# A hyena filter and a maxout feed-forward block: the down product of two tiles by Strassen's method

## The chip, the cores and the metric

The kernel runs on one core of one Trainium2 chip. Its time is the device time of one execution in microseconds. A profiled execution is read beside it: TensorE (PE) multiplies matrices, VectorE (DVE), ScalarE (ACT) and GpSimd (POOL) work elementwise, SyncE (SP) issues most of the DMAs.

## The reference

```python
# x, v: (4, 12544, 128); float32 throughout
h_mlp = np.maximum(pos_emb @ w1, 0.0) @ w2
h_filt = h_mlp * np.exp(-0.01 * np.arange(S))[:, None]
u = x * v
y = irfft(rfft(u, n=2*S, axis=1) * rfft(h_filt, n=2*S, axis=0)[None], n=2*S, axis=1)[:, :S]
t = (x * y).reshape(50176, 128)                 # d_model 128
h = np.maximum(np.maximum(t @ moe_w1, t @ moe_w2), t @ moe_w3)   # d_ff 768
out = h @ moe_w_out                             # (50176, 128)
```

A long convolution along the sequence, for each of four batches, gates `x`; every token then goes through a feed-forward block whose hidden layer is the maximum of three products.

## The kernel before

**The convolution** is a Fourier transform in steps, each a matrix product. The inputs of a batch come in 32 pieces (`u_load`, 128 x 392 of `xr` and of `vr`). A piece is multiplied on VectorE (`u_mul`), split into its 16-bit halves on GpSimd (`u_planes`, L356), turned by a transposing DMA (`u_dma`, tile `turned`), joined again on ScalarE and VectorE (`u_join`, tile `uT`) and multiplied by the first table (`u_first`, L141). Then come 45 pairs of frequencies: tables (`w_load`, tile `wt`) and the filter's spectrum (`h_load`, tile `ht`) are loaded, a second product is taken (`g_second`), VectorE and ScalarE form the sums and the products with the filter (`g_butterfly`, `g_swap`, `g_re`, L419, `g_im`, L423, whose last addition, L424, is on GpSimd, and `g_unfold`, L431), a third product follows (`g_third`), and its result goes to DRAM (`zd`, L450, issued by ScalarE).

**The feed-forward block** works on tiles of 392 tokens (`N`), 32 for each batch, 128 in all. `t_load` brings the tile's part of `zd` (tile `zt`) and of `x` (tile `xT`, four DMAs), `t_last` does the last product of the transform (`yps`) and multiplies by `x` (tile `gt`). Then there are six chunks of 128 hidden channels, one for each up step. The maximum of three is taken as relu of differences: the weights w2 and w3 have w1 subtracted, and what w1 itself contributes goes straight to the output through one 128x128 matrix, `lin`, which is w1 times w_out. An up step (`up`) is a product `pa`, a ReLU on ScalarE into `hid` (L545), a product `pb`, and a maximum on VectorE (L548); `pa` and `pb` turn through the three PSUM buffers of the pool `hps`. The down product (`down`) adds the chunk's share to `ops`; it follows one up step behind. After six chunks ScalarE copies `ops` out (L561) and issues the output's DMA (L563).

Every product is done in two halves of 64 output rows:

```python
    def halves_mm(out, lhsT, rhs, start, stop):
        for h in range(2):
            nc.tensor.matmul(out[64 * h:64 * h + 64], lhsT[:, 64 * h:64 * h + 64], rhs,
                             start=start, stop=stop, skip_group_check=True)
```

**The order** is written by hand; each engine keeps the order in which the program names its instructions. Batch 0 is transformed first, alone. Then the 32 x 6 = 192 up steps of batch b run with the convolution of batch b + 1 beside them: `conv_steps` gives each of its steps a slot, which is the number of an up step. With `per_pair` = 170/(45 + 0.6 x 32) = 2.65 slots, pieces are 1.59 slots apart and pairs of frequencies 2.65; the pieces take about the first 60 slots of a batch (for batch 1 six of them are done earlier), the pairs the others. A piece is loaded 10 slots before its `u_first`, multiplied 6, split 5 and turned 4 slots before, and joined just before. The last batch has nothing beside it.

SyncE's queue holds, in program order, `ut`, `turned`, `wt`, `ht`, `zt` and `xT`. The pieces' tiles come from two pools, `inp` (three buffers) and `inq` (two); `wt` has three buffers for each of its two tags, `ht` three, `uT` two; the convolution's products have four PSUM buffers (`cps`).

Of the kernel before, what the change touches and what calls it, by code (L numbers as in the profile page):

```python
# [9 lines left out]
FP32 = mybir.dt.float32  # L10
# [60 lines left out]
def kernel(  # L71
# [43 lines left out]
    w_sb = [const.tile([D, DFF], FP32, name=f"w_sb{i}") for i in range(3)]  # L115
    wo_sb = const.tile([P, NF, D], FP32, name="wo_sb")
    lin = const.tile([D, D], FP32, name="lin")
    eye = const.tile([P, P], FP32, name="eye")
# [104 lines left out]
    inp = ctx.enter_context(tc.tile_pool(name="inp", bufs=3))  # L223
# [3 lines left out]
    lwp = pro.enter_context(tc.tile_pool(name="lwp", bufs=3))  # L227
    fin = ExitStack()
# [20 lines left out]
    warm = sml.tile([P, 256], FP32, name="warm")  # L249
# [26 lines left out]
    def warm_up(n):  # L276

        ps = fps.tile([P, 1024], FP32, tag="cv", name="pw", bufs=2)
        for _ in range(n):
            halves_mm(ps[:, 0:256], warm[:, 0:P], warm[:], True, True)  # L280
# [34 lines left out]

    NU = NG
    us, uts, ws, hts, eos, xts, xss, abs_, pss = ({} for _ in range(9))

    def pools(b, u):
        if b == 0:  # L320
            return inp0 if u % 2 else inp
        return inp if u < EARLY or u % 5 < 3 else inq

    def u_load(b, u):
        c, g0 = divmod(u, NG // 4)
        ts = []
        for src in (xr, vr):
            t = pools(b, u).tile([P, 4, NB], FP32, tag=f"u{len(ts)}", name="ut")
            nc.sync.dma_start(
                t[:], src[4 * g0:4 * g0 + 4, :, c, b, :].rearrange("g p n -> p g n"))  # L330
            ts.append(t)
        us[u] = ts

    def u_mul(u):
        a, v = us[u]
        nc.vector.tensor_tensor(out=a[:], in0=a[:], in1=v[:], op=ALU.mult)  # L336
# [6 lines left out]
    def u_turn(u):  # L343
        if u % 2 == 0:
            uts[u] = uts[u + 1] = utp.tile([NB, 8, 2, 64], FP32, tag="uT", name="uT")
        ps = state["turn"].tile([P, 512], FP32, tag="cv", name="pst")
        turn(u, ps)
        nc.scalar.copy(uts[u][:, 4 * (u % 2):4 * (u % 2) + 4],
                       ps[0:NB, :].rearrange("n (s t r) -> n s r t", s=4, r=2))
# [3 lines left out]
    def u_planes(u):  # L353
        a, _ = us.pop(u)
        pl_ = planes[u % 3]
        nc.gpsimd.tensor_copy(  # L356
            pl_[:, :, :, 0:NB], a[:].bitcast(U16).rearrange("p s (n h) -> p h s n", h=2))
        us[u] = pl_

    def u_dma(u):  # L360
        t = hp.tile([P, 8, P], U16, tag="turned", name="turned", bufs=3)
        nc.sync.dma_start_transpose(
            out=t[:], in_=us.pop(u)[:].rearrange("p h s n -> p (h s n)"))
        us[u] = t

    def u_join(u):
        if u % 2 == 0:
            uts[u] = uts[u + 1] = utp.tile([NB, 8, 2, 64], FP32, tag="uT", name="uT")
        t = us.pop(u)
        for h in range(2):  # L370
            copies[h](
                uts[u][:, 4 * (u % 2):4 * (u % 2) + 4].rearrange(
                    "n s r t -> n (s r t)").bitcast(U16).rearrange(
                    "n (s r t h) -> n h s r t", h=2, r=2, t=64)[:, h],
                t[0:NB, 4 * h:4 * h + 4].rearrange("n s (t r) -> n s r t", r=2))
# [8 lines left out]
    def w_load(g, a):  # L384

        w = state["pair"][0].tile([P, 2, 2, P], FP32, tag=f"w{a}", name="wt")
        nc.sync.dma_start(w[:].rearrange("p k r m -> p (k r m)"), wt_d[g, :, a, :])
        ws[g, a] = w

    def h_load(g):  # L390
        ht = state["pair"][1].tile([P, 2, 2, 2, D], FP32, tag="h", name="ht")
# [18 lines left out]
    def g_swap(g):  # L410
        xt = xts[g]
        xs = state["cv"][0].tile([P, 2, 2, D], FP32, tag="xs", name="xs", bufs=2)
# [40 lines left out]
    def conv_steps(b, done):  # L453
# [4 lines left out]
        def at(slot, late, fn, *args):  # L458
            out.append((slot, late, len(out), fn, args))
# [14 lines left out]
        for g in range(NK):  # L474
            s = s0 + int(g * per_pair)
            at(s - 5, 0, w_load, g, 0)
            at(s - 3, 0, h_load, g)
# [16 lines left out]
    zts, xTs, gs, pos_, obs = ({} for _ in range(5))  # L494
# [18 lines left out]
    def t_last(i):  # L513
        zt = zts.pop(i)
        ps = cps.tile([P, 512], FP32, tag="cv", name="yps")
        g = hp.tile([D, 4, NB], FP32, tag="g", name="gt", bufs=2)
# [23 lines left out]
    def up(i, f):  # L540
        rhs = gs[i][:].rearrange("d p n -> d (p n)")
        h = hp.tile([P, N], FP32, tag="hid", name="hid")
# [8 lines left out]
    def down(i, f, h):  # L551
        if f == 0:
            pos_[i] = ops.tile([D, 512], FP32, tag="ops", name="ops")
            halves_mm(pos_[i][:, 0:N], lin[:], gs[i][:].rearrange("d p n -> d (p n)"), True,
                      False)
        halves_mm(pos_[i][:, 0:N], wo_sb[:, f, :], h[:], False, f == NF - 1)
        if f < NF - 1:
            return
        gs.pop(i)
        o = op_.tile([D, 4, NB], FP32, tag="o", name="ot")  # L560
        nc.scalar.copy(o[:].rearrange("d p n -> d (p n)"), pos_.pop(i)[:, 0:N])  # L561
        dst = outT.rearrange("d (p b n) -> d p b n", b=B, n=NB)[:, 4 * i[1]:4 * i[1] + 4, i[0], :]
        nc.scalar.dma_start(dst, o[:])  # L563
# [24 lines left out]
    def turn2(u):  # L588

        t = utp.tile([NB, 8, 2, 64], FP32, tag="uT", name="uT")  # L590
# [3 lines left out]
        nc.scalar.copy(t[:], ps[0:NB, :].rearrange("n (s t r) -> n s r t", s=8, r=2))  # L594
# [6 lines left out]
    warm_up(30)  # L601
# [56 lines left out]
    state = {"cv": (cvp, cps), "turn": cps, "xb": 2}  # L658
# [91 lines left out]
    hp = ctx.enter_context(tc.tile_pool(name="hp", bufs=3))  # L750
    f4p = hp.tile([N1, 2, NB // 2], FP32, name="f4p", bufs=1)
    nc.scalar.dma_start(f4p[:], f4p_d)
    inq = ctx.enter_context(tc.tile_pool(name="inq", bufs=2))
    planes = [hp.tile([P, 2, 4, P], U16, name=f"planes{i}", bufs=1) for i in range(3)]
    for t in planes:
        nc.gpsimd.memset(t[:].rearrange("p h s n -> p (h s n)"), 0)
    op_ = ctx.enter_context(tc.tile_pool(name="op", bufs=2))
    wp = ctx.enter_context(tc.tile_pool(name="wp", bufs=3))
    hh = ctx.enter_context(tc.tile_pool(name="hh", bufs=3))
    cvp = ctx.enter_context(tc.tile_pool(name="cvp", bufs=3))  # L760
    cps = ctx.enter_context(tc.tile_pool(name="cps", bufs=4, space=PSUM))
    hps = ctx.enter_context(tc.tile_pool(name="hps", bufs=3, space=PSUM))
    ops = ctx.enter_context(tc.tile_pool(name="ops", bufs=1, space=PSUM))
    state = {"turn": cps, "pair": (wp, hh), "cv": (cvp, cps), "xb": 3}


    tiles = [(b, i) for b in range(B) for i in range(NT)]
    late = None
    for n, (b, i) in enumerate(tiles):
# [4 lines left out]
        if n == 0:  # L774
            t_load(*tiles[0])
            t_load(*tiles[1])
            t_last(tiles[0])
        for f in range(NF):

            if i < NT - 2:  # L780
                if f == 0:
                    t_load(*tiles[n + 2])
            elif i == NT - 1 and f < 2 and n + 1 + f < len(tiles):
                t_load(*tiles[n + 1 + f])
            h = up((b, i), f)
            if late is not None:
                down(*late)
            late = ((b, i), f, h)
            if f == 3 and n + 1 < len(tiles):
                t_last(tiles[n + 1])  # L790
            s = i * NF + f
            run(beside.pop(s, ()))
            if s == NT * NF - 1:
                assert not beside, sorted(beside)
    down(*late)


# [35 lines left out]
```

## Time and profile before

| | us |
|---|---|
| median of 3 runs | 2412.57 |
| lowest and highest | 2412.53, 2420.22 |
| the profiled execution | 2411.47 |
| its span, first to last instruction | 2409.3 |

The first batch's transform, the filter and the weights take about the first 320 us; then come three batches of tiles with a convolution beside them, and from about 1960 us on the last batch alone. In a row of the page's groups stand the line, the engine, the operation, output and inputs with their shapes and the count; behind the bar the busy time in us and the mean of one instruction in ns, then the idle time of the engine before these instructions and what ended most of it. A product of float32 tiles appears as two matmul instructions for each half, so one `halves_mm` is four instructions; their durations overlap each other. A timeline row holds the start, the duration, the engine (SPq and ACTq are the queues from which DMAs are issued), the line and the tile. A row of windows holds the busy time of each engine in a stretch, then TensorE's granted clock, the mean busy share of the DMA engines and GB/s.

### The profile page before, as it was taken

Reading aid. Unit: us, or ns where it says so; the run is one execution under the profiler, and the core shown is the slowest. Engines: PE = TensorE matmul, PEld = TensorE weight load, DVE = VectorE, ACT = ScalarE, POOL = GpSimd, SP = SyncE. Lnnn points to the kernel's source line nnn. Section 1 sums busy time; section 2 is a strip of 40 time slices with the busy share of each in tenths; the row PEclk is TensorE's granted clock in tenths of the full one; section 3 lists DMA queues with packets and bytes.
Section 4 is the critical chain, followed back from the end, with each engine's and each line's share of the span. In section 5 each row is a group of like instructions: output and inputs, shape, how many; then the busy total and the mean of one; then the engine's idle time right before and its main releaser. Section 6 shows DMA issues by size and latency. Waiting matters only on the chain.

```text
span 2409.3 us, 63290 instructions
## 1 busy us (share of the span) xinstructions
PE 2393.4 (99%) x26089; PEld 1463.2 (61%) x26089; DVE 1286.4 (53%) x2719; ACT 1026.7 (43%) x1981; POOL 314.2 (13%) x349
## 2 busy tenths in 40 slices
PE   9999999999999999999999999999999999999999
PEld 8988866655555556666656546666665654444444
DVE  5588834466666645446666644446666642222222
ACT  2688834444444434444444424444444432222222
POOL 2022211011111101101111111101111100000000
PEclk9999999999999999999999999999999999999999
DMA  7778879767767659967777859968777742222221
GB/s 171 179 240 266 278 167 179 162 190 196 214 194 211 175 125 187 182 174 207 219 207 215 219 124 182 189 162 213 214 215 209 215 113 61 55 62 53 64 53 36
DMA packets 544553, 408.21 MB, mean 169 GB/s; under 512 B 390244, under 2 KB 436381, under 8 KB 544265
## 3 DMA queue, kind: packets, MB, share of 16 engines
q1 hardware_dynamic: 421760, 315.25, 53.8%
q10 hardware_dynamic: 117129, 74.31, 10.7%
q0 software_dynamic: 5376, 14.62, 2.1%
q8 instruction: 205, 3.36, 0.6%
q14 instruction: 83, 0.68, 0.1%
HBM read 295.76 MB, written 84.67 MB: 158 GB/s over the span
## 4 chain that ended last, share of the span: by engine, by line
PE 97%; DMA 1%; ACT 1%; DVE 0%; issue 0%; SPq 0%; ACTq 0%; POOL 0%; DVEq 0%
PE ops L132 24%; PE pb L132 21%; PE pa L132 21%; PE ps L132 13%; PE ps L141 7%; PE yps L132 5%; PE sps L688 3%; PE pm L303 1%; PE gps L674 1%; PE pst L341 1%; PE pw L132 1%; DMA hd<-ht 1%; ACT ht L693 0%; DMA xT<-in_x_dram 0%; DVE xt L424 0%
## 5 line engine op out<-in xcount | busy, mean ns | idle before, releaser
L548 DVE TENSOR_TENSOR hid<-hid,pb 128x392 f32<-128x392 f32 x768 | 431.8, 562 | 789.4 <-PE pb L132 510.2
L545 ACT ACTIVATE hid<-pa 128x392 f32<-128x392 f32 x768 | 381.9, 498 | 799.3 <-PE pa L132 630.1
L132 PE MATMUL pa<-gt,w_sb 128*64 128x392 f32 x3072 | 640.7, 493 | 1.1 <-DVE gt L533 1.1
L132 PE MATMUL pb<-gt,w_sb 128*64 128x392 f32 x3072 | 639.6, 492 | 1.4 <-ACT hid L545 1.2
L132 PE MATMUL ops<-hid,wo_sb 128*64 128x392 f32 x3072 | 639.5, 492 | 0.1
L132 PEld LDWEIGHTS pb<-gt,w_sb 128*64 128x64 f32 x3072 | 225.8, 137 | 283.0 <-issue 257.1
L132 PEld LDWEIGHTS ops<-hid,wo_sb 128*64 128x64 f32 x3072 | 227.1, 137 | 278.9 <-issue 228.8
L424 POOL TENSOR_TENSOR xt<-xt,xs 128x512 f32<-128x512 f32 x135 | 172.5, 1278 | 969.6 <-DVE xs L423 778.7
L132 PEld LDWEIGHTS pa<-gt,w_sb 128*64 128x64 f32 x3072 | 201.8, 137 | 111.3 <-issue 67.4
L141 PEld LDWEIGHTS ps<-f,uT 98*64 98x64 f32 x4096 | 178.0, 137 | 47.4 <-issue 44.7
L132 PEld LDWEIGHTS ps<-ab,wt 128*64 128x64 f32 x2880 | 168.4, 137 | 52.4 <-issue 26.8
L132 PE MATMUL ps<-ab,wt 128*64 128x128 f32 x2880 | 190.9, 274 | 1.8 <-DVE ab L431 1.7
L132 PEld LDWEIGHTS ps<-spec,wt 128*64 128x64 f32 x2880 | 168.0, 137 | 37.8 <-issue 34.2
L132 PE MATMUL ps<-spec,wt 128*64 128x128 f32 x2880 | 189.5, 273 | 1.4 <-issue 1.4
L141 PE MATMUL ps<-f,uT 98*64 98x90 f32 x4096 | 188.0, 241 | 0.0
L449 DVE TENSOR_TENSOR zs<-ps,z 128x256 f32<-128x256 f32 x270 | 102.0, 419 | 96.6 <-ACT z L447 94.3
L413 ACT ACTIVATE xs<-xt 64x512 f32<-64x512 f32 x180 | 113.1, 628 | 71.1 <-DVE xt L158 58.9
L431 DVE TENSOR_TENSOR ab<-xt 128x256 f32<-128x256 f32 x360 | 136.0, 419 | 1.6
L419 DVE TENSOR_TENSOR xt<-xt,ht 128x512 f32<-128x512 f32 x180 | 124.2, 690 | 15.6 <-ACT ht L693 15.2
L356 POOL COPY planes<-ut 128x784 uint16<-128x784 uint16 x90 | 76.2, 847 | 426.5 <-DVE ut L336 301.1
L145 ACT COPY spec<-ps 128x360 f32<-128x360 f32 (+1 forms) x132 | 71.8, 546 | 137.0 <-PE ps L141 136.8
L132 PEld LDWEIGHTS yps<-f4p,zt 90*64 90x64 f32 x3072 | 107.3, 138 | 34.4 <-issue 32.3
(86 smaller groups left out, 1824.4 us busy)
## 6 DMA issues: line engine op xcount, KB each, us to landing
wt<-wt_const SPq DMA_DIRECT2D x360, 256.0 KB, 4.8
ht<-hd SPq DMA_DIRECT2D x270, 256.0 KB, 4.5
zd<-zs ACTq DMA_DIRECT2D x180, 256.0 KB, 4.6
zt<-zd SPq DMA_DIRECT2D x192, 180.0 KB, 3.8
ut<-in_xr_dram SPq DMA_DIRECT2D x128, 196.0 KB, 3.6
ut<-in_vr_dram SPq DMA_DIRECT2D x128, 196.0 KB, 4.3
xT<-in_x_dram SPq DMA_DIRECT2D x512, 49.0 KB, 3.0
out_dram<-ot ACTq DMA_DIRECT2D x128, 196.0 KB, 4.0
```

The costliest lines, as they stand in the source:

```text
L132: nc.tensor.matmul(out[64 * h:64 * h + 64], lhsT[:, 64 * h:64 * h + 64], rhs, start=start, stop=stop, skip_group_check=True)
L141: nc.tensor.matmul(ps[64 * c:64 * c + 64, 256 * i + r * N1:256 * i + (r + 1) * N1], a[:, r, :], table[:, c * N1:(c + 1) * N1], start=(i % ...
L145: copy(dst, ps[:].rearrange("p (s m) -> p s m", m=256)[:, :, 0:2 * N1].rearrange("p s (r k) -> p k r s", r=2))
L356: nc.gpsimd.tensor_copy(pl_[:, :, :, 0:NB], a[:].bitcast(U16).rearrange("p s (n h) -> p h s n", h=2))
L413: nc.scalar.mul(xs[0:64], xt[64:128], -1.0)
L419: nc.vector.tensor_tensor(out=xt[:], in0=xt[:], in1=hts[g][:, 0], op=ALU.mult)
L424: (nc.gpsimd if apart else nc.vector).tensor_tensor(out=xt[:], in0=xt[:], in1=xs[:], op=ALU.add)
L431: nc.vector.tensor_tensor(out=ab[:, :, q, :], in0=y[:, :, 0, :], in1=y[:, :, 1, :], op=op)
L449: nc.vector.tensor_tensor(out=zs[:, a], in0=ps[:, 0:256], in1=z1[:], op=op)
L545: nc.scalar.activation(h[:], pa[:, 0:N], Relu)
L548: nc.vector.tensor_tensor(out=h[:], in0=h[:], in1=pb[:, 0:N], op=ALU.max)
L688: nc.tensor.matmul(ps[64 * h:64 * h + 64, (2 * c + k) * 2 * D:(2 * c + k + 1) * 2 * D], G[:, k, c], w2x[:].rearrange("p s d -> p (s d)"), ...
```

## The change

Two neighbouring tiles of a batch become a pair, and the down product of the pair is taken as a product of 2x2 blocks: the two tiles and the two halves of the 768 hidden channels on one side, the two halves of the hidden channels and of the 128 outputs on the other. Strassen's method, in Winograd's form, takes seven block products where the plain way takes eight. A block product is three chunks (`NC`), each with 64 output channels and 392 tokens; the two halves of the tokens, 196 each, go to the two halves of the output rows (`mm`). What `lin` contributes is added in four products of the same size. So a pair has 25 entries (`products`), spread evenly over twelve up steps, beginning nine up steps (`LAG`) after the pair's first.

The sums of hidden blocks (`s1` to `s4`, twelve instructions of 128 x 392 for each pair) are done on GpSimd. The sums of weights (`tw`, `linx`) are done once, on VectorE. The results of the seven products are combined from two PSUM buffers by two copies on ScalarE and five additions on VectorE of 128 x 196; each quarter of the output is stored by two DMAs, so eight for each pair in place of two, issued by ScalarE one step after it is formed.

To make room, buffers are shared: `wt` and the pieces `ut` share the tags of `inq`, `ht` takes the tag of `uT`, the split pieces and the turned ones take the tags `x` and `xs` of the frequency pairs (three buffers each), the padding of the split pieces is cleared for each piece, `cps` has three buffers in place of four, and `h_load` stands two slots later. `inp`, `eye` and the first weight are given up after the prologue. The name `inq` is bound twice, first to a pool of five buffers, then to one of two; the functions read the name when they are called, which is after both.

The twelve up steps of a pair alternate between the two tiles (`ORDER`). Both tiles of the next pair are loaded in steps 0 and 1 and transformed in steps 5 and 8; at a change of batch in steps 6 and 7, 9 and 11.

```diff
     def pools(b, u):
         if b == 0:
             return inp0 if u % 2 else inp
-        return inp if u < EARLY or u % 5 < 3 else inq
+        return inp if b == 1 and u < EARLY else inq
...
     def u_planes(u):
         a, _ = us.pop(u)
-        pl_ = planes[u % 3]
+        pl_ = cvp.tile([P, 2, 4, P], U16, tag="x", name="planes", bufs=3)
+        nc.gpsimd.memset(pl_[:, :, :, NB:].rearrange("p h s n -> p (h s) n"), 0)
...
     def u_dma(u):
-        t = hp.tile([P, 8, P], U16, tag="turned", name="turned", bufs=3)
+        t = cvp.tile([P, 8, P], U16, tag="xs", name="turned", bufs=3)
...
     def w_load(g, a):
-        w = state["pair"][0].tile([P, 2, 2, P], FP32, tag=f"w{a}", name="wt")
+        w = inq.tile([P, 512], FP32, tag=f"u{a}", name="wt")
...
     def h_load(g):
-        ht = state["pair"][1].tile([P, 2, 2, 2, D], FP32, tag="h", name="ht")
+        ht = utp.tile([P, 1024], FP32, tag="uT", name="ht")[:].rearrange(
+            "p (c k q d) -> p c k q d", c=2, k=2, q=2)
...
-            at(s - 3, 0, h_load, g)
+            at(s - 1, 0, h_load, g)
...
-    def down(i, f, h):
-        if f == 0:
-            pos_[i] = ops.tile([D, 512], FP32, tag="ops", name="ops")
-            halves_mm(pos_[i][:, 0:N], lin[:], gs[i][:].rearrange("d p n -> d (p n)"), True,
-                      False)
-        halves_mm(pos_[i][:, 0:N], wo_sb[:, f, :], h[:], False, f == NF - 1)
...
+    ORDER = (("h11", 0), ("h21", 0), ("h11", 1), ("h22", 0), ("h21", 1), ("h11", 2),
+             ("h21", 2), ("h22", 1), ("h22", 2), ("h12", 0), ("h12", 1), ("h12", 2))
+    BUFS = {"h11": 3, "h21": 4, "h22": 4, "h12": 3}
+    LAG = 9
+
+    def sum_(out, a, b, op):
+        nc.gpsimd.tensor_tensor(out=out[:], in0=a[:], in1=b[:], op=op)
...
+    SUMS = {2: (s3, 0), 4: (s2, 0), 5: (s3, 1), 7: (s3, 2), 8: (s2, 1), 9: (s2, 2),
+            10: (s1, 0), 11: (s1, 1), 12: (s1, 2), 13: (s4, 0), 14: (s4, 1), 15: (s4, 2)}
...
+        def mm(ps, w, rhs, start):
+            for c in range(2):
+                nc.tensor.matmul(ps[64 * c:64 * c + 64, 0:H2], w,
+                                 rhs[:, H2 * c:H2 * c + H2], start=start, stop=True,
+                                 skip_group_check=True)
...
+        plan = (
+            (X, "h11", wo_sb[:, 0:NC, 0:64], True, None, [(copied, "p1", X)], None),
+            (Y, "s2", tw[:, 0], True, None, [(added, "u2", "p1", Y)], None),
+            (X, "h12", wo_sb[:, NC:, 0:64], False, (m1, first), [(copied, "c11", X)],
+             (stored, 0, 0, "c11")),
+            (Y, "s3", tw[:, 1], False, (m2, second_), [(added, "u3", "p1", Y)], None),
+            (X, "h21", wo_sb[:, 0:NC, 64:128], True, None, [(added, "c22", "u3", X)],
+             (stored, 1, 1, "c22")),
+            (Y, "h22", tw[:, 2], True, (linx[:], second_), [(added, "c21", "u3", Y)],
+             (stored, 1, 0, "c21")),
+            (X, "h12", wo_sb[:, NC:, 64:128], False, (m2, first), [(added, "c12", "u2", X)],
+             (stored, 0, 1, "c12")),
+        )
...
     hp = ctx.enter_context(tc.tile_pool(name="hp", bufs=3))
+    inq = ctx.enter_context(tc.tile_pool(name="inq", bufs=5))
     f4p = hp.tile([N1, 2, NB // 2], FP32, name="f4p", bufs=1)
     nc.scalar.dma_start(f4p[:], f4p_d)
     inq = ctx.enter_context(tc.tile_pool(name="inq", bufs=2))
...
-    cps = ctx.enter_context(tc.tile_pool(name="cps", bufs=4, space=PSUM))
+    cps = ctx.enter_context(tc.tile_pool(name="cps", bufs=3, space=PSUM))
...
+            if j == 0:
+                entries = products(b, i, h, X, Y)
+                for q, e_ in enumerate(entries):
+                    at_ = step + LAG + q * NSTEP // len(entries)
```

## The prediction

> **What bounds the kernel now.** I read the page's busy times first, then the chain that ended last, then the costliest groups.
>
> ```profile
> span 2409.3 us, 63290 instructions
> ...
> PE 2393.4 (99%) x26089; PEld 1463.2 (61%) x26089; DVE 1286.4 (53%) x2719; ACT 1026.7 (43%) x1981; POOL 314.2 (13%) x349
> ...
> PE 97%; DMA 1%; ACT 1%; DVE 0%; issue 0%; SPq 0%; ACTq 0%; POOL 0%; DVEq 0%
> PE ops L132 24%; PE pb L132 21%; PE pa L132 21%; PE ps L132 13%; PE ps L141 7%; PE yps L132 5%; PE sps L688 3%; PE pm L303 1%; PE gps L674 1%; PE pst L341 1%; PE pw L132 1%; DMA hd<-ht 1%; ACT ht L693 0%; DMA xT<-in_x_dram 0%; DVE xt L424 0%
> ...
> L424 POOL TENSOR_TENSOR xt<-xt,xs 128x512 f32<-128x512 f32 x135 | 172.5, 1278 | 969.6 <-DVE xs L423 778.7
> ```
>
> The reader is to see that TensorE carries the whole chain, and that the down product (`ops`) is the largest piece of it. Work taken off TensorE comes off the time, as long as nothing else is then late. So I looked next for what is nearly late already, by the windows, over one stretch in which the convolution's inputs are loaded (886 to 1032 us) and over the last batch, which has no convolution beside it.
>
> ```profile
> core 0: us, PE busy (x) PEld busy (x) DVE busy (x) ACT busy (x) POOL busy (x), PEclk, DMA share, GB/s
> ...
> 886.00:1032.00 146.00, 146.00 (x1792) 87.45 (x1790) 71.33 (x145) 61.36 (x116) 26.12 (x31) 1.00 0.98 183
> ...
> 2000.00:2400.00 400.00, 400.00 (x3196) 189.89 (x3194) 116.97 (x208) 103.58 (x209) 0.00 (x0) 1.00 0.21 56
> ```
>
> In the loading stretch TensorE is busy for all 146 us, but the DMA engines are at 0.98 too. The timeline of SyncE there shows that its queue has no room either:
>
> ```profile
> 950.29 0.58 SPq L329 DMA_DIRECT2D ut<-in_xr_dram  x1
> 950.92 0.51 SPq L329 DMA_DIRECT2D ut<-in_vr_dram  x1
> 951.59 1.24 SPq L362 DMA_TRANSPOSE turned<-planes  x1
> 952.87 0.58 SPq L329 DMA_DIRECT2D ut<-in_xr_dram  x1
> ```
>
> Rows follow each other without a gap, and VectorE's multiplication at 954.23 waits for the load issued at 950.92. Loads arrive just in time. This is the stage to fear.
>
> **What is removed and added on TensorE.** In the last batch a 392-column product (four matmul instructions) starts every 0.66 us (2302.37, 2303.03, 2303.69). Two tiles now take 12 down products and 2 `lin` products: 14 x 0.658 = 9.21 us. After the change they take 21 + 4 = 25 products of 196 columns. No row has 196 columns; the neighbours are 0.658/392 = 1.68 ns a column at 392, 0.219/128 = 1.71 at 128 (16 instructions of `ps<-spec` in 0.875 us), 1.36/8/98 = 1.73 at 98, and 0.92/8/49 = 2.35 at 49, where weight loads show. 196 lies between 128 and 392, so I take 1.70: 0.333 us each, 8.33 us. The saving is 0.88 us a pair; at 1.73 ns it would be 0.73, at the ideal 1.5 x 0.658 it is 0.99. Over 64 pairs: **56.6 us**, between 47 and 63. All of it lies on the path.
>
> **GpSimd's sums.** 12 of 128x392 for each pair. The nearest row is L424, 1278 ns for 512 columns: 1278 x 392/512 = 0.98 us, 11.7 us a pair, where a pair takes 25 us without and about 33 us with the convolution beside it. With the 1.28 us add of each frequency pair, every 2.65 steps, and a copy of 0.85 us for each loaded piece, GpSimd is about half busy, and no sum is needed before two steps after its issue: s2 of the third chunk, the tightest, is issued at step 9 and read at step 11. Free by itself. But the sums get in the way of others. The timeline (start and duration in us):
>
> ```profile
> 489.10 1.27 POOL L424 TENSOR_TENSOR xt<-xt,xs 128x512 f32<-128x512 f32 x1 [35.09 <-PE pb L132]
> ...
> 489.56 1.35 DVE L419 TENSOR_TENSOR xt<-xt,ht 128x512 f32<-128x512 f32 x1
> ```
>
> The same in the view of the tile `xt` from 350 to 1850 us (count, then shortest, median and longest in ns):
>
> ```profile
> L419 DVE TENSOR_TENSOR xt<-xt,ht x122: 681/684/1353, 484.2 to 1849.5; 128x512 f32<-128x512 f32 x122
> ```
>
> The one multiplication of two SBUF tiles that starts inside a GpSimd add takes 1353 ns in place of 684 and ends 0.54 us after the add. VectorE instructions with one input in PSUM (L158, 0.41 us) run beside the same adds at their usual length. So a collision costs VectorE about 0.67 us.
>
> Of these instructions there are four for each frequency pair, 1.5 a step. If GpSimd is busy half the time, half of them meet it: 0.75 x 0.67 = 0.5 us a step. VectorE is at 62% in that stretch (199 of 323 us, 1.74 us of a step of 2.82); with 0.5 and the five short additions (about 0.3 us each, half of L548's 0.56, 0.13 us a step) it comes to 2.37 of 2.74 us. That still fits, and there is a cushion: a step's maximum (L548) is done 1.9 us into its step, and its `hps` buffer is wanted again two steps, 5.7 us, after the step's start, so VectorE may be 3.8 us late. I charge 8 us for steps where several collisions fall together; bounds 0 and 47, the latter under the rivals.
>
> The Trainium skill speaks against the change here: "GPSIMD Engine Reference", section 8 "Key points", says that GpSimd shares its SBUF interfaces with VectorE and contends with instructions that read two SBUF inputs. If that rule is taken to mean that every meeting blocks VectorE for the whole sum, 0.98 in place of the 0.67 of the row, VectorE would be at 2.6 of 2.74 us, and by my estimate the 8 us would be 25 and the sum 2412.
>
> **The loads.** The new first binding of `inq`, five buffers, holds no tile; every `ut` and `wt` tile comes from the second one, of two. In the built program 84 of the 90 `ut` loads wait for a GpSimd instruction, the copy (L356) of the piece two before. So two pieces go through load, multiply, copy, and only then is the next issued. Queued behind the waiting load on SyncE are the transposes, `zt` and `xT`, `ht` and `wt`; TensorE waits for these through `t_last`, VectorE through the multiplication, and behind that the maxima. The cycle, from the rows at 950: xr issued at 950.29, multiplied at 954.23, copied until 956.23, 5.94 us for two pieces, 2.97 each. With one collision (0.67) and a sum ahead of the copy (0.98) it is 7.6, 3.8 each. Now a piece costs SyncE 2.8 us (950.29, 952.87, 955.90). A piece comes every 1.59 steps (`conv_steps`), so twelve steps hold 7.55 pieces, and two tile loads (`zt` and `xT`), which fill SyncE for some 6.5 us each (941.89 alone shows 6.13 us for four `xT`). Before: 7.55 x 2.8 + 13 = 34.1 us, where TensorE takes 146/50.8 x 12 = 34.5 (32 pieces are 50.8 steps). After: TensorE 33.6; loads, with 1.5 us of cycle hidden behind the tile loads, 33.9 at 2.97, 37.2 at 3.4 and 40.2 at 3.8. A loading stretch is 4.2 times that: 0, 15 or 28 us late for each batch. Between issue and use lie four steps, 11 us, of which a landing takes 4 (median 3.7 in this stretch), and VectorE has its 3.8 us; if all of that is still there, some 10 us a batch are absorbed, if the queue is as full as at 950, nothing. Three batches: 0 to 15 us at the low and middle cycle with slack, 45 at the middle without, 83 at the worst. I take the middle cycle and about half the slack, **25 us**.
>
> **What goes beside other work.** Output stores rise from 2 to 8 for each pair: 384 more issues on ScalarE at 0.39 us, 150 us. ScalarE is at 43%, and a ReLU, done 1.2 us into its step, is missed only by `pb` of the next step, 2.3 us later; so nothing, unless an issue waits for an older transfer: SyncE shows such waits, `xT` for `out_dram` 65.2 us in 24. The 90 small memsets (240 of 1024 elements of a row of 971 ns, 0.23 us) run while GpSimd waits for the product. `wt` from three buffers to two and `ht` from three to the two of `uT` only bind SyncE to what TensorE has already done; it has gaps there. Three `cv` banks in place of four hold at most one or two at a time.
>
> **Ends.** Two tiles must be loaded and transformed before the first up step, in place of one: 3 us, the issue time of its `zt` (0.89) and `xT` (2.0). At each change of batch the second tile is needed one step after it is made: 0 to 4 us, three times, I take 4 in all. Together 7.
>
> **Sum.** The profiled execution took 2411.47 us (span 2409.3; the median of the runs is 2412.57, 1.1 above). 2411.5 - 56.6 + 25 + 8 + 7 = **2395 us**.
>
> **Rivals.** (a) Everything is hidden: the cycle stays at 2.97 and the slack is there. 2411.5 - 56.6 + 4 = 2359. For it: SyncE never waited long for GpSimd so far. Against: no gap in its queue. (b) The saving is eaten almost exactly: losses between 50 and 64 us, 2405 to 2419. (c) Slower: the two load buffers become the bound. Two pieces in 7.6 us and no slack: 83 us; 2411.5 - 56.6 + 83 + 8 + 7 = 2453. It wins from about 3.5 us a piece on with an already full queue, and the DMA share of 0.98 speaks for it. (d) Slower: VectorE becomes the bound. If every one of the 1.5 instructions a step meets a sum, 1.0 us is added and a step takes 1.74 + 0.13 + 1.0 = 2.87 us of VectorE against 2.74 of TensorE: 0.13 x 360 steps = 47 us in place of the 8, 2434. Only one collision in 122 stands in the trace, so it has little for it but the number of sums.
>
> **How the numbers follow.** Forecast (2370 to 2404) 0.33, (a) 0.17, (b) 0.13, (c) 0.25, (d) 0.12. 0.3%, 7 us, is about what a measurement of this kernel can tell from no change. Faster: forecast and (a), 0.50; same: (b), 0.13; slower: 0.37. The range goes from just under (a) to just over (c), 2357 to 2455; the forecast's own is 2370 to 2404.
>
> **What would show it.** In the last batch, steps of 12 should be 0.9 us shorter with TensorE still at 100%; if not, the 1.70 ns are wrong. In the loading stretches SyncE's waits for `planes` should come up from 9 us to tens, with TensorE idle there; L419, L423 and L431 should have maxima near 1.3 us and a higher mean. If TensorE is full everywhere, (a) holds; if its idle time lies between the loading stretches, (d); if in them and over 20 us each, (c). I am wrong altogether if ScalarE's stores wait for SyncE's loads and hold up the ReLU.

## The result, and the profile after

The changed kernel takes 2481.74 us (median of 4 runs, 2479.15 to 2484.39) against 2414.55 us (2412.53 to 2420.22) of the kernel before, run beside it: ratio 1.0274, 95% interval 1.0251 to 1.0298. It is slower by 67 us, where 2395 us, a gain, was forecast; the longest time that the prediction reckoned with was 2455 us. The page of the profiled execution (2479.97 us, span 2476.6):

```profile
PE 2375.2 (96%) x29025; PEld 1667.2 (67%) x29025; DVE 1460.5 (59%) x3044; ACT 998.1 (40%) x1981; POOL 1115.7 (45%) x1204
...
PE 70%; DVE 9%; DMA 9%; ACT 5%; issue 4%; ACTq 2%; SPq 1%; POOL 0%; DVEq 0%
...
L435 POOL TENSOR_TENSOR xt<-xt,xs 128x512 f32<-128x512 f32 x135 | 172.5, 1278 | 476.5 <-DVE xs L434 355.8
```

TensorE fell from 99% to 96% busy, and its share of the chain from 97% to 70%: what ends last is now a mixture of VectorE, transfers, ScalarE and issues. No engine is full in place of TensorE. ScalarE is at 40%, VectorE at 59%, GpSimd at 45%: the time went into waits for each other. The windows show where, one over a loading stretch, one over frequency pairs and one over the last batch:

```profile
core 0: us, PE busy (x) PEld busy (x) DVE busy (x) ACT busy (x) POOL busy (x), PEclk, DMA share, GB/s
904.00:1055.00 151.00, 144.44 (x1986) 104.34 (x1982) 87.89 (x164) 58.59 (x113) 85.92 (x110) 0.99 0.87 176
1100.00:1423.00 323.00, 302.20 (x3462) 202.27 (x3460) 216.59 (x477) 128.99 (x278) 154.39 (x143) 0.99 0.74 200
2060.00:2440.00 380.00, 380.00 (x3826) 233.73 (x3824) 136.36 (x278) 96.69 (x205) 175.95 (x176) 1.00 0.25 59
```

With no convolution beside it TensorE is full as it was (380 of 380), although GpSimd does its sums there for 176 us. With it, TensorE idles: for 6.6 of 151 us, and for 20.8 of 323 where the kernel before was busy for 322.4. The starts of the `pa` products in TensorE's timeline give each group of twelve up steps its time. Change against before, summed over stretches of a batch, in us:

| batch | steps 0-12 | 12-60, loads | 60-180, frequency pairs | 180-192 |
|---|---|---|---|---|
| 0 | -3.1 | +0.2 | +18.1 | -1.4 |
| 1 | +0.2 | +5.0 | +24.3 | -1.0 |
| 2 | 0.0 | +3.2 | +24.7 | -0.3 |

The last batch, from its first step to its last, goes from 427.3 to 411.5 us. The first step starts 4.4 us later (323.6 against 319.2), and from the last step's start to the span's end there are 15.6 us in place of 6.9. TensorE's own saving would give -14 in each batch, so each of the first three lost 28 to 42 us against it: 27 to 34 in the frequency-pair stretch (whose share of the saving is some 9) and 4 to 9 in the loading stretch. 13 us are lost at the ends. The excess to be explained is 2482 against 2358 (2415 less the 56.6 of TensorE): 124 us.

Who makes TensorE wait, over the whole span (engine, line, what it waited for: us in total, times, longest), as PEld (its weight loads) and as PE:

```profile
PEld pb L131 <- ACT hid L556: 108.1, 137, 3.7
...
PE pb L131 <- ACT hid L556: 39.8, 49, 3.0
...
PEld ps L131 <- DVE ab L442: 38.9, 63, 1.4
...
PE ps L131 <- DVE ab L442: 21.3, 38, 1.0
```

`pb` waits for the ReLU, which frees its `hps` buffer. In the kernel before, the first two of these rows were 17.8 us in 49 and 1.2 us in 2. The chain that ended last has five places where a store stands behind a `zd` transfer, 35.5 us with the transfers' own time. One of them (start, duration):

```profile
1203.75 7.88 DMA zd<-zs
...
1211.71 0.62 ACTq L624
...
1212.36 0.62 ACTq L624
...
1213.03 0.51 ACT hid L556
...
1213.58 1.32 PE pb L131 x4
```

ScalarE's next instruction is an output store, it waits for an older `zd` transfer, then two stores are issued at 0.62 us each, and only behind them stands the ReLU for which TensorE waits. Such waits stand in the kernel before too. A transfer reports its end through a semaphore, a counter that several transfers use in turn, and a store first waits for the older transfer with its semaphore: in the trace 477 of the 512 stores do, and 104 of the 128 of the kernel before. Nearly all find it landed. The waits held ScalarE's queue in 10 places, 26.9 us in all and 6.3 at most, nearly all of it for `zd`; in the kernel before in one, for 1.0 us.

### The profile page after: what moved, and what is told of

Same layout as the page of the kernel before. It is cut to its first block, busy times and chain, and to the rows that moved or that the text cites. A ratio compares the mean times of both kernels' runs of the same rounds, so it can differ in the third digit from the quotient of the medians.

```text
span 2476.6 us, 71313 instructions
## 1 busy us (share of the span) xinstructions
PE 2375.2 (96%) x29025; PEld 1667.2 (67%) x29025; DVE 1460.5 (59%) x3044; ACT 998.1 (40%) x1981; POOL 1115.7 (45%) x1204
## 4 chain that ended last, share of the span: by engine, by line
PE 70%; DVE 9%; DMA 9%; ACT 5%; issue 4%; ACTq 2%; SPq 1%; POOL 0%; DVEq 0%
PE ops L605 16%; PE pb L131 15%; PE pa L131 15%; PE ps L131 8%; PE ps L140 7%; PE yps L131 4%; PE sps L775 3%; DMA zd<-zs 2%; DVE ab L442 2%; DMA ht<-hd 2%; DVE zs L460 2%; ACT hid L556 2%; DMA out_dram<-o 1%; ACT xs L425 1%; DVE xs L434 1%
## 5 line engine op out<-in xcount | busy, mean ns | idle before, releaser
L131 PEld LDWEIGHTS pb<-gt,w_sb 128*64 128x64 f32 x3072 | 219.2, 137 | 343.6 <-issue 222.1
L605 PE MATMUL ops<-hid,wo_sb 128*64 128x196 f32 x3072 | 335.9, 332 | 1.0 <-DVE hid L559 1.0
L575 POOL TENSOR_TENSOR s<-hid 128x392 f32<-128x392 f32 x192 | 202.3, 1054 | 256.4 <-DVE hid L559 248.9
L575 POOL TENSOR_TENSOR s<-hid,s 128x392 f32<-128x392 f32 x192 | 199.0, 1037 | 142.5 <-DVE hid L559 141.2
L575 POOL TENSOR_TENSOR hid<-hid,s 128x392 f32<-128x392 f32 x192 | 200.1, 1049 | 91.9 <-DVE hid L559 72.3
L131 PE MATMUL ps<-ab,wt 128*64 128x128 f32 x2880 | 197.5, 276 | 21.7 <-DVE ab L442 21.3
L131 PEld LDWEIGHTS ps<-ab,wt 128*64 128x64 f32 x2880 | 162.4, 136 | 53.3 <-DVE ab L442 38.9
L575 POOL TENSOR_TENSOR hid<-hid 128x392 f32<-128x392 f32 x192 | 194.3, 1031 | 0.0
L442 DVE TENSOR_TENSOR ab<-xt 128x256 f32<-128x256 f32 x360 | 174.9, 526 | 1.6
L605 PE MATMUL ops<-s,tw 128*64 128x196 f32 x1536 | 171.7, 329 | 0.0
```

Source lines behind the costliest of these rows:

```text
L442: nc.vector.tensor_tensor(out=ab[:, :, q, :], in0=y[:, :, 0, :], in1=y[:, :, 1, :], op=op)
L575: nc.gpsimd.tensor_tensor(out=out[:], in0=a[:], in1=b[:], op=op)
L605: nc.tensor.matmul(ps[64 * c:64 * c + 64, 0:H2], w, rhs[:, H2 * c:H2 * c + H2], start=start, stop=True, skip_group_check=True)
```

## The experiments

Theories at the outset: A, the stores on ScalarE hold up the ReLU; B, the two load buffers; C, the GpSimd sums hold up VectorE. Later came D (ScalarE is late because what it copies is late), E (the wait for `g`) and F (three `cv` banks). Each run is shown with its median, and its ratio to the kernel before on the same chip, whose median was between 2414.0 and 2416.8.

### One suspect taken from the changed kernel

Five load buffers, and no sums:

```
# five buffers: the second binding goes
-    inq = ctx.enter_context(tc.tile_pool(name="inq", bufs=2))
# no sums: s2 like s3, s1 and s4 do nothing
-        h["s3", j] = hp.tile([P, N], FP32, tag="s3", name="s3", bufs=3)
-        sum_(h["s3", j], h["h11", j], h["h21", j], ALU.subtract)
+        h["s3", j] = h["h21", j]
```

> The changed kernel with the second binding of inq taken out, so that u, v and wt tiles come from five buffers in place of two. The excess to be explained is 124 us: 2482 against the 2358 that the TensorE saving alone (2415 less 56.6) would give; about 30 us of it lie in the loading stretches of batches 1 to 3, about 80 in their frequency-pair stretches, 13 at the ends. Theory B (two load buffers): the loading stretches come back to TensorE's pace, 2450, and if late loads also feed the rest, down to 2375. Theories A (stores on ScalarE) and C (sums against VectorE): 2470 to 2482, at most 10 us less.

> The changed kernel without its twelve GpSimd sums of each pair; the products read the unsummed hidden tiles, so the values of the output are those of other operands while every TensorE product, copy and store is kept. Theory C: 80 to 110 us come back, 2375 to 2400, and the additions and multiplications of two SBUF inputs return to 684 and 418 ns. Theory A: 2455 to 2480, as the stores are all there. Theory B: 2450 to 2470, since the copies that free load buffers no longer queue behind sums. Together: 2400 to 2440.

Five buffers: 2458.18 us, ratio 1.0175 (1.0160 to 1.0191), 23.5 us less. No sums: 2462.15 us (2452.91 to 2471.35), 1.0201 (1.0161 to 1.0240), 19.5 less. The four runs without sums lie in two pairs, at 2453 and 2471 us, so that gain is somewhere between 10 and 29 us. Both take part, neither is the whole. With five buffers SyncE no longer waits as it did; in the changed kernel its largest wait for another engine during the convolution, and its wait in the loading stretch, were

```profile
SPq L396 <- PE ps L131: 289.5, 90, 7.5
...
SPq L337 <- POOL planes L365: 64.0, 50, 6.2
```

and with five the first is 5.4 us in 15. L396 is the load of `wt`: that, and not `ut`, looks like the dearer part of the two buffers, though no run gave one of them more buffers without the other. The loading stretches of batches 1 and 2 gave back 6 us of the 24 (from 5.0 and 3.2 to 1.2 and 0.8), their frequency-pair stretches 17 (from 24.3 and 24.7 to 13.9 and 17.8); that of batch 0 lost 3 (from 18.1 to 21.4).

What the sums did to VectorE stands in the view of the tile `xt` of the changed kernel, 350 to 1850 us (count, then shortest, median and longest in ns):

```profile
L442 DVE TENSOR_TENSOR ab<-xt x224: 407/418/1264, 494.1 to 1841.9; 128x256 f32<-128x256 f32 x112
...
L430 DVE TENSOR_TENSOR xt<-xt,ht x114: 676/684/1528, 487.3 to 1848.7; 128x512 f32<-128x512 f32 x114
```

Without the sums the longest are 421 and 693 ns: the collisions are the sums. They cost up to 0.84 us each (1528 less 684). From 330 to 1950 us 78 of the 375 instructions of these two kinds are longer, by 0.63 us on average, so the prediction's row of 0.67 us was the better price, and the strict reading of the rule set beside it (the Trainium skill, "GPSIMD Engine Reference", section 8), a whole sum of 1.03 to 1.05 us, is not reached. Without the sums VectorE is busy for 1374.4 us in place of 1460.5. Little of the cost is GpSimd's queue: SyncE waits 60.9 us for `planes` without the sums and 64.0 with them, and TensorE's weight loads wait for sums for some 3 us in all.

### The sums, the banks and the stores put into the kernel before

```
# sums: one in each up step
+            nc.gpsimd.tensor_tensor(out=w_sb[0][:, 0:N], in0=w_sb[1][:, 0:N],
+                                    in1=w_sb[2][:, 0:N], op=ALU.add)
# split stores
-        nc.scalar.dma_start(dst, o[:])
+        for m in range(2):
+            for c in range(2):
+                nc.scalar.dma_start(dst[64 * m:64 * m + 64, 2 * c:2 * c + 2],
+                                    o[64 * m:64 * m + 64, 2 * c:2 * c + 2])
# ScalarE copies, after each store
+        for _ in range(4):
+            nc.scalar.copy(w_sb[0][:, 0:480], w_sb[1][:, 0:480])
# three banks
-    cps = ctx.enter_context(tc.tile_pool(name="cps", bufs=4, space=PSUM))
+    cps = ctx.enter_context(tc.tile_pool(name="cps", bufs=3, space=PSUM))
```

> The kernel before, with one GpSimd addition of 128x392 in each up step (from two weight tiles to one that nobody reads), as many as the changed kernel's sums; no instruction waits for it except those behind it on GpSimd. Theory C (collisions of VectorE with sums cost time by themselves): 2435 to 2465. Theory A: 2413 to 2420, since VectorE has slack when ScalarE is on time. The prediction's own step for this was 8 us, between 0 and 47.

> The kernel before with three cv banks of PSUM for the convolution in place of four, the number that the changed kernel has. Theory F: 2430 to 2460, the part that the three suspects did not explain. Theory E, and the prediction's own step, which priced it at nothing: 2413 to 2420.

> The kernel before, with the output store of each tile split in four of 64 partitions and 2 x 98 columns, as the changed kernel issues them: eight for two tiles, all on ScalarE. Nothing else is changed. Theory A: most of the excess appears here too, 2480 to 2520. Theories B and C: within 10 us of 2415. Together: 2415 to 2435, because VectorE is still early enough here.

> The kernel before, with its output stores as they are and four more ScalarE copies of 128x480 after each tile's store, from a weight tile to one that nobody reads: by the row of 0.62 us for 512 columns some 0.58 us each, 2.3 us a tile, about what the split stores added to ScalarE's queue in the run with split stores (four of 0.69 us less one of 0.39, 2.4 us). Theory A1 (the stores cost by the time that ScalarE is occupied): as slow as that run, 2510 to 2550. Theory A2 (they cost by their waits for older transfers, which ScalarE's queue then serves in order): ScalarE's time alone is absorbed, 2415 to 2440.

Sums: 2415.85 us, ratio 1.0000 (0.9991 to 1.0010), although the longest L431 rose from 422 to 1237 ns. But as many sums met VectorE less often here. The additions that form `ab`, first in this run, then in the changed kernel (mean of 419 ns in the kernel before):

```profile
L431 DVE TENSOR_TENSOR ab<-xt 128x256 f32<-128x256 f32 x360 | 139.7, 429 | 1.6
...
L442 DVE TENSOR_TENSOR ab<-xt 128x256 f32<-128x256 f32 x360 | 174.9, 526 | 1.6
```

VectorE is busy for 28 us more than before (1314.3 against 1286.4), where the sums of the changed kernel add 86. So that many collisions cost nothing where ScalarE and the transfers are on time; that three times as many would is not shown. Three banks: 2413.14 us, 0.9995 (0.9985 to 1.0004), theory F falls.

Split stores: 2546.96 us, 1.0538 (1.0520 to 1.0556), 131 us slower. ScalarE copies: 2532.25 us, 1.0489 (1.0473 to 1.0504), 115 slower, with not one transfer more. The copies took 0.59 us each. So ScalarE's time alone is enough (A1). Waits for older transfers (A2) held ScalarE's queue for 1.2 us in all in the run with split stores, so they are not the 16 us between the two runs; what is stays open. The timeline of ScalarE with split stores, in the last batch, shows a step that the prediction thought free:

```profile
2155.77 0.48 ACT L561 COPY ot<-ops 128x392 f32<-128x392 f32 x1 [0.82 <-PE ops L132]
2156.28 2.58 ACTq L565 DMA_DIRECT2D out_dram<-ot  x4
2158.96 0.89 ACT L545 ACTIVATE hid<-pa 128x392 f32<-128x392 f32 x2 [2.71 <-DMA out_dram<-ot]
```

Two ReLUs come late together. The last row names a transfer, but the four issues fill 2.58 of its 2.71 us. These two runs are no measure of the changed kernel's own loss: they put four issues or copies in a row and so lose time in the last batch too (453.3 and 453.9 us against 427.3), where the changed kernel, with two in a row, loses none.

### Other places for the stores

```
# on GpSimd; the run on SyncE has nc.sync
-                nc.scalar.dma_start(
+                nc.gpsimd.dma_start(
# the layout
-            dst = outT.rearrange("d (p b n) -> d p b n", b=B, n=NB)
+            dst = outT.rearrange("d (b p n) -> d b p n", b=B, n=NB)
# four stores: the layout, and one store for each quarter in place of the two
+            nc.scalar.dma_start(
+                dst[64 * m:64 * m + 64, b, p0:p0 + 4].rearrange("d (c p) n -> c d (p n)", c=2),
+                t[name][:])
```

> The changed kernel with its eight output stores of each pair issued by GpSimd instead of ScalarE; nothing else. Theory A (512 issues of 0.62 us on ScalarE, and their waits for older transfers, hold up the ReLU): 80 to 110 us come back, 2375 to 2400, and the rows where pb waits for the ReLU nearly vanish. Theory C (sums against VectorE): no better, since GpSimd has more in its queue: 2475 to 2500. Theory B (load buffers): no better either, or worse, since the copies that free the buffers are on GpSimd: 2480 to 2510. If A and C only act together (ScalarE and VectorE wait for each other in turn), 40 to 80 us come back: 2400 to 2440.

> The changed kernel with its eight output stores of each pair issued by SyncE instead of ScalarE. Theory A: the frequency-pair stretches come back, but some of it is lost again in the loading stretches, where SyncE's queue is full: 2425 to 2455. Theory D: 2480 to 2510, since each load behind a store is later still.

> The changed kernel with the four quarters of an output pair stored by one DMA each in place of two: 128 partitions, four issues a pair, not eight. For this the output lies batch by batch in memory, so a store's run is 784 bytes and not 392. Theory A: about half of what the stores cost comes back, 30 to 50 us, 2430 to 2450, more if an issue of 128 partitions takes 0.39 us again and not 0.62. Theories B and C: 2470 to 2482.

> The changed kernel with both repairs: u, v and wt tiles from five buffers, and four output stores a pair of 128 partitions each. If the two costs add up, the 24 us that five buffers alone gave come off the time of the run with four stores: 2405 to 2430, about the kernel before. If late loads were only late because ScalarE was (its stores and the loads wait for each other), less than 12 us. A version that beats both kernels needs the sums' 20 us as well, or the end's 13.

> The changed kernel with eight stores a pair as it has them, but with the output batch by batch in memory, as the run with four stores had it (runs of 784 bytes in place of 392). It tells whether that run was slower for the layout or for its 128-partition stores. If the layout is the reason: 2505 to 2520. If the stores' form is: 2470 to 2485.

GpSimd: 2509.17 us, 1.0381 (1.0362 to 1.0400), 27 us slower than the changed kernel. An issue takes 622 ns there too, 317 us in all, and the mean of L430 (500 to 1800 us) rises from 786 to 1122 ns. As GpSimd and VectorE are slower for it, this run says little on ScalarE. SyncE: 2467.99 us, 1.0221 (1.0205 to 1.0236), 14 us faster than the changed kernel and slower than theory A gave. With no store left on ScalarE the row of `pb`'s weight loads that wait for the ReLU is still 93.3 us in 123, of 108.1 in 137. So that row names the last link of a chain, and most of it is not the time of the stores on ScalarE.

Four stores of 128 partitions: 2514.12 us, 1.0408 (1.0387 to 1.0429), 32 us slower, against every theory that was written. With five buffers besides, 2499.21 us, 1.0353 (1.0336 to 1.0370), so the buffers gave 15 us there and not 24. The layout alone: 2483.21 us, 1.0290 (1.0272 to 1.0307), no change. So it was the form of the stores. ScalarE's issues fell to 0.53 us each, half as many, and its waits for stores all but vanished, but transfers were late: `uT` waited 97.4 us for transposes in place of 55.1, `ht` came late by 37.6 in place of 9.8. Among the longest 195 pieces of the chain eight are output transfers of 6.3 us on average, against 12 of 3.2 with the layout alone. The Trainium skill has a rule that would explain it ("DMA: Bandwidth & Descriptors", "Rules for kernel authors"): the outermost dimension of either side limits how many of the 16 DMA engines a transfer uses, and on the DRAM side it is here `c`, of size two. The trace agrees. ScalarE's queue with the layout alone, then with four stores (packets, MB, share):

```profile
q10 hardware_dynamic: 90505, 74.33, 10.3%
...
q10 hardware_dynamic: 82825, 74.30, 9.8%
```

The stores' data makes 32,768 packets in both. The 7,680 packets that are missing are of 4 bytes: the trace has 16 of them for each of the 512 stores, and 2 for each of the 256. If each engine closes its part with one, as these numbers suggest, a store of the four used two engines. That this is what made the transfers late fits, and is not shown: no run had four stores over sixteen engines.

### All suspects away, and the wait that was left

```
# two of eight stores
-            for c in range(2):
+            for c in range(name in ("c11", "c22")):
# t_last later
-        lasts = (9, 11) if turn_ else (5, 8)
+        lasts = (9, 11) if turn_ else (7, 10)
```

> The changed kernel with only two of its eight output stores for each pair (half of c11 and half of c22), so three quarters of the output are left unwritten; copies, additions and products are all kept. Theory A (the stores' time on ScalarE, as the run with extra ScalarE copies supports): 2395 to 2425, so 57 to 87 us come back. Theory D (ScalarE is late because what it copies is late: transposes, loads and VectorE; the run with four stores spoke for that): 2460 to 2482.

> The changed kernel with all three suspects taken away: two of eight stores a pair (three quarters of the output unwritten), no GpSimd sums (the products read unsummed hidden tiles), u, v and wt tiles from five buffers. If these three are the whole excess, TensorE's saving less the ends remains: 2360 to 2380. If something else of the change costs time (two buffers for ht, three cv banks, the order of the products), more than 2390.

> The changed kernel with t_last of the next pair at steps 7 and 10 of a pair in place of 5 and 8. Its g takes one of four buffers, and in the changed kernel the buffer of the first is still to be read by a lin product of a step later, so that VectorE's multiplication waits for TensorE (125 us of idle time in the run without all three suspects, up to 4.2 us each), with every maximum behind it. With the steps moved it waits for its own yps alone. Theory E (this wait is the part that the three suspects did not explain): 20 to 45 us come back, 2437 to 2462. Theory F (three cv banks in place of four, or something else): 2475 to 2485.

> The run without all three suspects (two of eight stores, three quarters of the output unwritten; no GpSimd sums, so unsummed operands; five load buffers), which took 2414, and t_last at steps 7 and 10 besides. Theory E: TensorE's saving shows, 2360 to 2380. Theory F: 2400 to 2414.

Two of eight stores: 2443.46 us, 1.0121 (1.0106 to 1.0136), 38 us less, between A and D; the stores are the largest single piece. Without all three suspects: 2414.04 us, 0.9996 (0.9987 to 1.0006). The whole saving was still missing, so something else stood there. The view of the tile `gt` in that run, 330 to 1950 us, names it (what the instructions that write or read `gt` waited for, then who waited for them: us, times):

```profile
its engine sat idle before it (us, times) until:
...
  PE ops L603: 125.5, 39
...
  PE yps L131: 19.1, 28
...
who waited for it (us, times):
...
  DVE gt L546: 83.4, 27
  DVE gt L544: 42.1, 12
```

It is VectorE's multiplication by `x` that waits for `ops`, 83.4 + 42.1 = 125.5 us. It should wait for `yps` alone, as in the kernel before (67.2 us in 74, no row for `ops`). `gt` has four buffers, two pairs. The 25 products of a pair begin at its step 9, so the first tile's `gt` is last read at step 9 + 24 x 12 // 25 = 20, the second's at 9 + 9 = 18: steps 8 and 6 of the next pair. But that next pair calls `t_last` at its steps 5 and 8. In the changed kernel's trace all of these waits are for the product with `linx`, the last reader of the second tile, at step 6. The view of the tile `linx`, who waited for it (us, times):

```profile
  DVE gt L546: 99.4, 38
  DVE gt L544: 37.1, 12
```

So the call at step 5 gets the second tile's buffer, a step before it is free; the one at step 8 does not wait for a buffer. VectorE, which works in order, stands up to 4.6 us before the multiplication, with the maxima behind it.

`t_last` at steps 7 and 10: the group `PE ops` is gone (`PE yps`, 25.3 us in 32, is all that is left), and the time is 2456.34 us, 1.0178 (1.0162 to 1.0193), 25.4 less. With the three suspects away as well it is 2368.71 us, 0.9813 (0.9798 to 0.9828): 45 us by that one line, and the page shows the kernel that the prediction had in mind.

```profile
PE 2339.3 (99%) x29025; PEld 1664.3 (70%) x29025; DVE 1376.0 (58%) x3044; ACT 1004.8 (42%) x1981; POOL 333.8 (14%) x436
```

The four pieces taken singly make 23.5 + 19.5 + 38.3 + 25.4 = 107 us, together 113 of the 124. Of the 11 that remain some 6 are at the ends: in this run the first step starts 3.7 us later, and 9.5 us follow the last step's start in place of 6.9. The rest lies in the frequency-pair stretches, where the two `ht` buffers and the order of the products were not tried singly.

### Repairs that keep the computation

```
# all three: five buffers and t_last at 7 and 10, as above; then three repairs
+                nc.sync.dma_start(
# or half
+                (nc.scalar, nc.sync)[c].dma_start(
# or nc.sync, and two steps later
-                            later(at_ + 1, *fn)
+                            later(at_ + 3, *fn)
```

> The changed kernel with three repairs that keep its computation: five load buffers (24 us by their run), stores issued by SyncE (14 us by theirs), t_last at steps 7 and 10 (20 to 45 us under theory E). If they add up: 2400 to 2424, at or just below the kernel before. Under theory F 2440 to 2445.

> The changed kernel with five load buffers and t_last at steps 7 and 10, and of each pair's eight stores four issued by ScalarE and four by SyncE. With all eight on SyncE it took 2426, and SyncE's ht loads and xT loads were late behind stores (VectorE waits for ht 32 us in all). If the place of the issues is a question of how full a queue is, half on each costs less than either: 2405 to 2422. If each store costs the same wherever it is, 2424 to 2435.

> The changed kernel with five load buffers, t_last at steps 7 and 10, all stores on SyncE, and each store two steps later in the program. In the run with three repairs SyncE waited for the copies and additions that make a store's data, 46 us in all, with the loads behind it. If that is what makes ht late: 2405 to 2420. If it is the stores' waits for older transfers (68 us, zd above all), no change: 2422 to 2430.

Three repairs: 2426.21 us, 1.0047 (1.0030 to 1.0064). The singles would give 2482 - 24 - 14 - 25 = 2419, so they nearly add up. Half of the stores on each queue: 2412.32 us, 0.9993 (0.9983 to 1.0002). All on SyncE but two steps later: 2406.03 us, 0.9961 (0.9947 to 0.9975), 9 us faster than the kernel before and the only version with the full computation that beats both. The wait of VectorE for `ht`, 31.6 us in 20 with three repairs, is then

```profile
DVE xt L430 <- DMA ht<-hd: 12.1, 6, 3.0
```

A store that waits for its data in a queue of loads makes the loads late: SyncE's waits of stores for VectorE's additions fell from 22.1 to 1.8 us. A store on SyncE is not free even so: its waits for `zd` remain at 48.4 us in 16, of 67.8 in 25.

## Why the prediction was wrong

**TensorE's saving: right.** 25 entries at 0.333 us were forecast; the drain after the last up step shows 80 instructions, 20 entries, in 6.66 us. Groups of twelve steps of the last batch go from 26.9 to 26.0 us, the forecast 0.9.

**The stores, priced at nothing: the step that failed most.** It reckoned that a ReLU is missed only by the `pb` of the next step, 2.3 us later, and charged nothing "unless an issue waits for an older transfer". Beside the convolution that did not hold. An issue of 64 partitions takes 0.62 us (shortest 602 ns), not the 0.39 of the row of 128 partitions (384 ns), so two in a row are 1.24 us; ScalarE also has the `zd` stores, which wait for VectorE, and the copies between a ReLU and its turn. Waits for an older transfer held the queue for 27 us in ten places besides. The run with ScalarE copies shows that time alone suffices to hold up the ReLU; the run with two stores puts the loss at 38 us. How much of the 38 is time of issue and how much these waits is not shown. In the last batch the 2.3 us were enough. The prediction named nearly this (stores that wait for SyncE's loads) as its own refutation and gave it no case and no chance.

**The wait for `g`: not in the prediction at all.** The prediction asked for the loads and the sums where the change adds a wait, not for `gt`, whose four buffers and lagging last reader stand in the change. Alone 25 us, 45 with the rest repaired.

**The loads: right sum, wrong place.** +25 was forecast, 23.5 was measured; that they agree is luck. The cycle of `ut`, load, multiply, copy, which the forecast priced, gave some 6 us in the loading stretches; the waits of SyncE for GpSimd rose from 9 to 64 us, but most of that TensorE did not feel. The balance itself counted waits as work: the row of 6.13 us for four `xT` loads holds them, while one issue takes 0.43 us. SyncE's timeline there, full in the kernel before, has gaps:

```profile
1018.20 0.52 SPq L337 DMA_DIRECT2D ut<-in_xr_dram  x1
1018.77 0.54 SPq L337 DMA_DIRECT2D ut<-in_vr_dram  x1
1019.42 1.24 SPq L371 DMA_TRANSPOSE turned<-planes  x1
1021.36 0.38 SPq L337 DMA_DIRECT2D ut<-in_xr_dram  x1
```

The rest came, as far as the waits tell, from `wt`, of which the prediction said that two buffers "only bind SyncE to what TensorE has already done; it has gaps there". SyncE stood 289.5 us in 90 such waits, with `ht` and the tile loads queued behind.

**GpSimd's sums: mis-sized.** +8 between 0 and 47 was forecast, 19.5 measured (10 to 29). A sum takes 1.03 to 1.05 us, not 0.98, and the price of a collision was about right (0.63 us on average, 0.67 forecast). Collisions were fewer than reckoned: 0.5 us in each of some 360 steps would be 180 us of VectorE, and 86 were added. What was mis-sized must then be what a late VectorE costs: the cushion of 3.8 us was taken as whole, while waits for `g` alone took up to 4.6 us of it. VectorE was never full (rival d; 217 of 323 us in the pairs' window), it was late. **The small pieces**: three `cv` banks at nothing was right; the ends cost 13 us, not 7. Of these, 8.7 lie behind the last step; they stay when six of eight stores are left out (15.6 us follow its start as before), and shrink without the sums (12.4, and 9.5 with two of eight stores besides). What holds the end there stays open.

**The rivals.** None gave 2482. The largest was 2453, for the load buffers; the worst case of one mechanism was taken as the worst case of all. Five costs of 13 to 38 us fell together, and the forecast had nothing for the two largest.

The common fault is a way of reading: busy shares were used to say that work is free. What decided was the order in a queue. With TensorE's `pb` one ReLU from waiting, each thing put in front of the ReLU on ScalarE, or of the maximum on VectorE, can count as soon as the neighbours' slack is used up.

## What to carry to other kernels

Where TensorE is full and three engines feed it in order, price each added instruction by what is queued behind it, not by the engine's share of busy time, and count DMA issues by their measured time in that very form. For each tile that gets a lagging reader, work out the step at which it is last read and the step at which its buffer is written again. Before a change with several small costs is given up, take them away one by one: here four edits, none of which touched the saving, moved 2482 to 2406 us.

## What was not expected of the hardware

A store of 64 partitions and 49 KB holds its queue longer (0.62 us on ScalarE, SyncE and GpSimd alike) than one of 128 partitions and 196 KB (0.384 us). A VectorE addition of two SBUF inputs (`ab`) took up to 1264 ns in place of 418 in the kernel with the GpSimd sums, and 421 at most without them (350 to 1850 us); the 28 us that such collisions added to VectorE in the kernel before cost it nothing. Stores in half the number, 0.53 us each, made the kernel 32 us slower, and transfers beside them came later.
